# Stores issued from the ScalarE queue instead of the SyncE queue, in a recurrence with a highway layer behind it

## The chip, the cores and the metric

The kernel runs on one core of one Trainium2 chip. The metric is the device time of one launch in microseconds (us); less is better. A core has TensorE (PE in the profile), VectorE (DVE), ScalarE (ACT), GpSimd (POOL) and SyncE (SP), each with its own instruction stream that runs in order, and 16 DMA engines that move data between HBM and on-chip memory. A DMA is started by an instruction on some engine's stream; here that is SP or ACT.

## The reference

Two layers over 25344 tokens (4 sequences of 6336) of 256 channels, float32 in and out:

```python
sig = 1.0 / (1.0 + np.exp(-f_logit))
f = lower_bound + (1.0 - lower_bound) * sig
i = 1.0 - f
for t in range(S):                      # per sequence, per channel
    h = f[:, t] * h + i[:, t] * x[:, t]
    y[:, t] = h
# second layer, on y as (25344, 256)
H = np.maximum(y @ w_h, 0.0)
T = 1.0 / (1.0 + np.exp(-(y @ w_t + b_t)))
out = T * H + (1.0 - T) * y
```

Both inputs, `x` and `f_logit`, are read once and the output is written once: 26 MB each.

## The kernel before

The tokens are cut into 21 units, numbered 0 to 20, of 2 to 16 blocks of 128 tokens; a unit of 16 blocks has two halves of 8 (sub-tiles). Each block group goes through one chain:

- `l` and `x` load the logits and the inputs (1 MB for 8 blocks), into 5 buffers each (slots 0 to 4).
- `u` (ACT) is the sigmoid of the negated logits; `b`/`B` (POOL, in two cases DVE) multiplies it by `x`. A slot of `l` is free when its `u` is done, a slot of `x` when its product is done.
- `i` and `p` (PE) transpose both; `f` (ACT, in some cases DVE) makes the gate; `s` (DVE) is the scan over time.
- `z` and `g` (PE) are the two matrix products, `t` (ACT) the second sigmoid, `d` (DVE) and `e`/`E` (POOL or DVE) the gating.
- `o` (PE) puts the result for 4 blocks in PSUM, `c` (ACT, in three cases DVE) copies it to one of 4 buffers `o`, and `w` stores that buffer: 512 KB, in three cases 256 KB.

A token such as `w7.0.1` is the store of unit 7, chunk 0, half 1; `l11.1` is the load of the logits of unit 11, sub-tile 1; `:3` behind a token names its slot or bank. The whole order of the work is one string of tokens written by hand, and every engine runs its own tokens in that order. So the place of a `w` token sets where the store stands in the stream of the engine that issues it. `do_w` (L408) issues stores and `load` (L250) issues loads; both go to SP before the change, 51 stores and 58 loads on one queue.

The program gives every DMA one of eight completion counters, shown as DMAHW0 to DMAHW7, in turn over the DMAs of all queues. A DMA that takes a counter first waits until the DMA that had it before, eight DMAs earlier, has landed. We call the counters lanes.

Of the kernel before, what the change touches and what calls it, by code (L numbers as in the profile page):

```python
# [55 lines left out]
b4.0.0:1 o1.0.0:1 p3.0.0:5 k*4:6 s3.1:0 l6.0:1 c0.0.0:0 x6.0:1 i4.0.1:4 f4.1:0 b4.0.1 k*4:0 k*4:0 s3.0:1 i4.0.0:0
l7.1:2 g3.0.1:67 d2.0.1 e2.0.1 c1.0.0v:1 w1.0.0 d3.0.1:3 u5.0:1 i5.0.1:2 p4.0.0:1 B5.0:2 i5.0.0:3 z3.0.0:45 f4.0:3
f5.1:2 f5.0:1 g3.0.0:67 z3.0.1:23 t3.0.0:0 w0.0.0 x7.1:2 s4.0:2 p4.0.1:0 p5.0.0:1 o2.0.0:45 u6.0:2 d3.0.0 e3.0.0
l7.0:3 t3.0.1 x7.0:3 c2.0.0:2 i6.0.1:6 f6.1:3 s4.1:3 g4.0.1:23 p5.0.1:0 u7.1:3 e3.0.1v d4.0.1:0 o3.0.1:45 c3.0.1:3
z4.0.1:67 t4.0.1:1 o3.0.0:23 z4.0.0:45 s5.0:4 i6.0.0:1 b6.0.1:0 c3.0.0:1 t4.0.0 g4.0.0:67 s5.1:5 g5.0.1:23 d4.0.0  # L60
b6.0.0 p6.0.0:0 z5.0.1:67 l8.0:4 f6.0:0 u7.0:0 t5.0.1:2 w3.0.1 l8.1:0 b7.1.1:1 x8.1:4 d5.0.1:1 z5.0.0:45 s6.0:0 t5.0.0
i7.0.1:23 i7.1.1 f7.1:1 b7.1.0 e4.0.1 e4.0.0v p6.0.1:1 s6.1:1 w2.0.0 g5.0.0:67 x8.0:0 o4.0.0:45 c4.0.0:0 g6.0.1:23
u8.0:1 l9.1:1 o4.0.1:45 p7.1.1:01 d5.0.0 b7.0.0:2 d6.0.1:2 c4.0.1:3 b7.0.1 p7.0.1 l9.0:2 e5.0.0v i7.0.0:67 e5.0.1
w3.0.0 u8.1:2 i7.1.0 s7.1:2 f7.0:2 p7.0.0:45 p7.1.0 z6.0.0:23 x9.0:1 z6.0.1:67 t6.0.0:0 t6.0.1 i8.0.1:01 s7.0:3 i8.1.1
# [5 lines left out]
E7.1 d8.0.0:2 w6.0.0 w6.0.1 x10.0:4 s9.1:0 b10.1.1:2 o7.0.1:45 u10.0:1 b10.1.0 o7.0.0:67 c7.0.1:1 c7.0.0:2 i10.0.0  # L70
p9.1.0:45 p9.0.0 s9.0:1 z8.0.1:67 l11.1:0 o7.1.1:23 f10.0:0 l11.0:2 t8.0.1:0 c7.1.1:3 z8.1.1:01 b10.0.1:0 x11.1:0
w7.0.0 t8.1.1:1 i10.0.1:67 i10.1.1 o7.1.0:23 g8.0.1:01 w7.0.1 c7.1.0v:0 z8.1.0:45 d8.0.1 f10.1:3 x11.0:1 t8.1.0
b10.0.0 g9.1.1:23 z9.1.1:67 g9.0.0:45 w7.1.1 u11.1:3 d9.1.1:3 t9.1.1:2 z8.0.0:23 t8.0.0 u11.0:0 E8.1v d9.0.0:0
g9.0.1:01 d9.0.1 w7.1.0 p10.1.0:67 z9.0.0:45 p10.0.0 l12.0:1 e8.0.1 z9.0.1:23 e8.0.0v t9.0.0:1 t9.0.1 o8.1.1:01
c8.1.1:2 i11.0.1:45 i11.1.1 p10.1.1:23 p10.0.1 f11.1:2 o8.0.0:01 c8.0.0:1 s10.0:2 o8.0.1:67 b11.1.0:1 i11.0.0:45
b11.1.1 l12.1:3 i11.1.0 b11.0.0:2 c8.0.1:3 x12.1:2 b11.0.1 f11.0:1 s10.1:3 o8.1.0:01 u12.0:2 c8.1.0:0 e9.1.1 g9.1.0:67
d9.1.0 g10.1.1:23 d10.1.1:2 g10.0.0:45 d10.0.0:1 w8.1.1 e9.0.1 g10.1.0:67 d10.1.0 g10.0.1:23 u12.1:1 d10.0.1
z10.0.0:01 e9.0.0 t10.0.0:0 e10.0.0v p11.0.0:45 z10.0.1:67 t10.0.1 p11.1.0 o9.0.1:23 c9.0.1:2 z10.1.0:01 t10.1.0:1
x12.0:3 l20.0:4 b12.1.0:0 z10.1.1:67 t10.1.1 e10.0.1 w8.0.1 l13.0:0 w8.1.0 w8.0.0 i12.1.1:23 i12.0.1 f12.1:0 w9.0.1
l13.1:2 s11.0:4 p11.1.1:01 p11.0.1 e10.1.0v x13.0:4 e10.1.1 s11.1:5 o9.0.0:67 c9.0.0:3 w9.0.0 z9.1.0:45 o10.0.1:23  # L80
i12.0.0:67 t9.1.0 c10.0.1:0 i12.1.0 w10.0.1 b12.0.1:1 o10.0.0:45 b12.0.0 b12.1.1 f12.0:3 o10.1.0:23 c10.1.0:1
c10.0.0:2 g11.1.1:01 d11.1.1:0 g11.0.1:67 d11.0.1:1 e9.1.0 g11.0.0:23 d11.0.0 x13.1:0 w10.0.0 u13.0:3 b13.0.0:2
u13.1:0 b13.0.1 g11.1.0:01 o10.1.1:45 d11.1.0 p12.0.0:67 c10.1.1:3 p12.1.0 s12.0:2 z11.0.0:23 z11.1.1:01 o9.1.1:45
t11.1.1:0 t11.0.0:1 e11.0.0 p12.0.1:01 u20.0:2 p12.1.1 i13.0.0:23 i13.1.0 c9.1.1:0 l14.0:1 x14.0:1 f13.0:1 o9.1.0:67
l15.0:3 s12.1:3 w10.1.1 w9.1.1 b13.1.1:1 z11.1.0:45 i13.1.1:23 w10.1.0 t11.1.0 c9.1.0:2 l16.0:0 e11.1.1v i13.0.1
f13.1:2 w9.1.0 e11.1.0v z11.0.1:45 t11.0.1 b13.1.0 g12.1.0:67 d12.1.0:2 g12.0.0:01 u14.0:1 d12.0.0:3 e11.0.1
g12.1.1:23 z12.1.0:67 x15.0:3 p13.0.0:45 p13.1.0 t12.1.0:2 d12.1.1 z12.0.0:01 t12.0.0:0 z12.1.1:23 t12.1.1 b14.0.0:0
e12.1.1 o11.1.1:67 c11.1.1:3 x16.0:2 s13.0:0 e12.1.0 w11.1.1 o11.0.1:01 c11.0.1:0 p13.0.1:23 p13.1.1 i14.0.1:6 f14.1:3
w11.0.1 e12.0.0 o11.1.0:45 c11.1.0:1 s13.1:1 w11.1.0 z12.0.1:01 t12.0.1 o11.0.0:67 c11.0.0:2 g12.0.1:45 d12.0.1
o12.1.0:01 w11.0.0 i14.0.0:6 f14.0v:0 b14.0.1 u15.0:3 z13.0.1:23 t13.0.1:1 g13.1.1:45 u16.0:0 g13.0.1:67 b15.0.1:2  # L90
d13.1.1:0 z13.1.0:23 t13.1.0:2 o12.1.1:45 c12.1.1:3 x17.0:4 c12.1.0:0 d13.0.1:1 g13.1.0:67 l17.0:2 e12.0.1v o12.0.0:23
c12.0.0:1 e13.0.1v b15.0.0 p14.0.1:4 i16.0.1:5 b16.0.0:1 f16.1:1 p14.0.0:0 d13.1.0 e13.1.0 i15.0.1:1 f15.1:2 s14.1:4
l18.0:4 o12.0.1:67 c12.0.1:2 z13.1.1:23 s14.0:5 w12.0.1 t13.1.1 w12.1.0 w12.1.1 g13.0.0:45 i16.0.0:1 f16.0:3 e13.1.1
d13.0.0 z13.0.0:67 w12.0.0 p15.0.1:0 s15.1:2 z14.0.0:23 t13.0.0 i15.0.0:1 t14.0.0:0 g14.0.0:67 g14.0.1:45 d14.0.0:2
e13.0.0 d14.0.1 z14.0.1:23 p15.0.0:0 f15.0:0 b16.0.1 s15.0:3 u17.0:1 t14.0.1 i20.0.1:1 f20.1:2 o13.1.1:67 x18.0:0
E14.0v o13.0.0:45 c13.1.1:2 c13.0.0:0 o13.0.1:23 x19.0:1 g15.0.1:01 c13.0.1:3 u18.0:3 d15.0.1:3 B17.0:0 p16.0.1:6
g15.0.0:45 o13.1.0:23 d15.0.0 c13.1.0:1 i17.0.1:0 s16.1:0 w13.0.1 f17.1:0 p16.0.0:1 z15.0.1:45 z15.0.0:23 w13.0.0
t15.0.1:2 b18.0.1:2 t15.0.0 p17.0.1:0 o14.0.0:67 c14.0.0:3 s16.0:1 o14.0.1:45 c14.0.1:0 w13.1.1 i18.0.0:2 i17.0.0:1
f17.0:1 f18.0:3 l19.0:1 x20.0:3 g16.0.0:67 z16.0.0:45 t16.0.0:1 s17.1:4 u19.0:0 d16.0.0:1 g16.0.1:01 d16.0.1 p17.0.0:3
z16.0.1:67 E15.0 o15.0.0:45 o15.0.1:12 s17.0:5 w14.0.0 i20.0.0:0 f20.0v:0 w13.1.0 t16.0.1 c15.0.0:2 b18.0.0 p18.0.0:6  # L100
i18.0.1:7 c15.0.1:3 b20.0.0:1 f18.1:1 g17.0.0:45 z17.0.1:23 s18.0:2 z17.0.0:01 t17.0.1:0 d17.0.0:0 i19.0.0:6 p18.0.1:7
s18.1:3 t17.0.0 f19.0:3 E16.0 B19.0:0 g17.0.1:23 o16.0.0:45 c16.0.0:1 e17.0.0 w14.0.1 o16.0.1:01 c16.0.1:0 d17.0.1
g18.0.0:67 z18.0.0:45 t18.0.0:2 d18.0.0:2 p19.0.0:0 s19.0:0 w15.0.1 w15.0.0 i19.0.1:1 g18.0.1:23 f19.1:1 z18.0.1:67
p19.0.1:0 t18.0.1 w16.0.1 w16.0.0 p20.0.0:1 e17.0.1 d18.0.1 o17.0.0:45 o17.0.1:23 s19.1:1 g19.0.1:0 c17.0.0:3 w17.0.0
e18.0.0 e18.0.1v p20.0.1:4 c17.0.1:2 w17.0.1 d19.0.1:3 z19.0.1:5 o18.0.1:67 z19.0.0:0 s20.0:4 s20.1:5 t19.0.1:1
c18.0.1:0 t19.0.0 g19.0.0:1 w18.0.1 o18.0.0:23 c18.0.0:1 e19.0.1 d19.0.0 g20.0.1:4 z20.0.0:0 z20.0.1:1 t20.0.1:0
e19.0.0v t20.0.0 o19.0.0:67 w18.0.0 c19.0.0:3 g20.0.0:2 w19.0.0 d20.0.1:1 d20.0.0 e20.0.1 e20.0.0v o20.0.0:0 c20.0.0:2
w20.0.0
"""

    pool = ctx.enter_context(tc.tile_pool(name="sb", bufs=1))
# [296 lines left out]
    def do_w(eng, slot, n, q, r):  # L408
        j0, j1 = blocks(n, q, r)
        o = st[n]["o", q, r].rearrange("p (j d) -> p j d", d=D)  # L410
        pin(nc.sync.dma_start(rows(out, units[n][0], j0, j1), o[:, :j1 - j0]))
# [40 lines left out]
```

## Time and profile before

| | |
|---|---|
| time, median of 3 runs | 208.13 us (208.1 to 209.46) |
| the profiled execution | 208.83 us |
| its span, first to last instruction | 207.1 us |
| busy: PE, DVE, ACT, POOL | 194.7, 192.8, 190.9, 171.9 us |
| moved by DMA | 78.67 MB, mean 380 GB/s |
| granted TensorE clock | 1.0 throughout |

All times in the views below are us from the span's start, if no other unit is given. A row of the timeline gives start, length, engine, line, operation and the tiles that it writes and reads; "SPq" and "ACTq" are the instruction streams (sequencers) of those engines, whose waits and DMA issues are not counted as busy time. "x2" means two like instructions that follow each other, merged into one row with their joint length.

### The profile page before, as it was taken

What the parts mean: (1) busy time and instruction counts of PE and PEld (TensorE: products, weight loads), DVE (VectorE), ACT (ScalarE), POOL (GpSimd) and SP (SyncE); (2) the same over time, 40 slices, a digit from 0 to 9 for tenths busy, and PEclk for the clock granted to TensorE, in tenths of its full rate; (3) what the DMA queues carried; (4) which work ended last, traced back from release to release, by engine and by line L of the source; (5) the groups of instructions that cost most, each with busy time, mean ns of one, the idle gap of its engine ahead of it and who ended that gap; (6) DMA issues with size and microseconds to landing.
All of it is one profiled execution on the core that took longest, in us unless ns stands there. A gap on an engine that the chain in (4) does not pass through costs nothing.

```text
span 207.1 us, 4606 instructions
## 1 busy us (share of the span) xinstructions
PE 194.7 (94%) x1850; PEld 135.0 (65%) x1850; DVE 192.8 (93%) x141; ACT 190.9 (92%) x173; POOL 171.9 (83%) x90
## 2 busy tenths in 40 slices
...
GB/s 178 365 425 416 418 423 418 418 419 412 425 418 420 420 419 421 424 417 419 427 415 418 423 414 429 418 417 427 412 424 390 403 325 352 364 141 161 206 304 253
DMA packets 15980, 78.67 MB, mean 380 GB/s; under 512 B 1748, under 2 KB 2264, under 8 KB 10072
## 3 DMA queue, kind: packets, MB, share of 16 engines
q1 hardware_dynamic: 15952, 78.39, 93.5%
...
q14 instruction: 6, 0.05, 0.1%
...
## 4 chain that ended last, share of the span: by engine, by line
PE 48%; DVE 17%; ACT 16%; DMA 11%; issue 4%; POOL 2%; SPq 1%; DVEq 0%; ACTq 0%
PE psum L333 13%; PE psum L145 11%; DMA l<-in_f_logit_dram 11%; DVE y L320 10%; PE psum L393 6%; DVE d L363 6%; PE psum L394 6%; ACT f L301 6%; PE psum L286 6%; PE psum L311 5%; ACT u L262 4%; ACT t L356 3%; ACT o L405 2%; POOL bv L277 2%; DVE f L299 1%
## 5 line engine op out<-in xcount | busy, mean ns | idle before, releaser
L277 POOL TENSOR_TENSOR bv<-u,x 128x1024 bf16<-128x1024 f16 (+2 forms) x44 | 99.8, 2293 | 18.3 <-ACT f L301 7.4
L320 DVE TENSOR_TENSOR_SCAN y<-f,y,psum 128x1024 bf16<-128x1024 f16 (+6 forms) x40 | 103.7, 2614 | 1.0 <-ACT f L301 0.6
L377 POOL TENSOR_TENSOR d<-d,t 128x1024 bf16<-128x1024 bf16 (+3 forms) x35 | 71.7, 2063 | 11.4 <-ACT t L356 6.1
L333 PE MATMUL psum<-y,w_sb 128*128 128x512 bf16 (+1 forms) x224 | 77.4, 367 | 3.0 <-ACT f L301 1.9
L145 PE MATMUL psum<-y,w_sb 128*128 128x512 bf16 x184 | 69.7, 379 | 0.7 <-DVE y L320 0.7
L363 DVE SCALAR_TENSOR_TENSOR d<-y,ncc,psum 128x1024 bf16<-128x1024 bf16 (+2 forms) x56 | 62.6, 1147 | 3.4 <-PE psum L145 1.5
L356 ACT ACTIVATE t<-psum,bt 128x1024 bf16<-128x1024 f32 (+2 forms) x56 | 56.3, 1038 | 2.6 <-PE psum L145 1.7
L262 ACT ACTIVATE u<-l 128x2048 f16<-128x2048 f32 (+2 forms) x28 | 48.6, 1747 | 5.4 <-DMA l<-in_f_logit_dram 5.4
L301 ACT ACTIVATE f<-psum,ncc 128x1024 f16<-128x1024 f16 (+3 forms) x38 | 50.9, 1365 | 1.6 <-PE psum L286 1.6
L405 ACT COPY o<-psum 128x1024 f32<-128x1024 f32 (+1 forms) x49 | 48.5, 1031 | 2.2 <-PE psum L394 1.0
L393 PE MATMUL psum<-diag,y 128*128 128x128 f16 x396 | 48.8, 219 | 0.6 <-ACT f L301 0.4
L394 PE MATMUL psum<-ident_b,d 128*128 128x128 bf16 x396 | 48.6, 219 | 0.8 <-DVE d L377 0.8
L394 PEld LDWEIGHTS <-d 128*128 128x128 bf16 x396 | 44.0, 113 | 4.8 <-DVE d L377 1.2
L393 PEld LDWEIGHTS <-y 128*128 128x128 bf16 x396 | 44.2, 113 | 2.5
L333 PEld LDWEIGHTS <-w_sb 128*128 128x128 f16 x224 | 21.6, 98 | 18.1 <-issue 1.0
L145 PEld LDWEIGHTS <-w_sb 128*128 128x128 f16 x184 | 17.9, 97 | 21.3 <-issue 6.0
L311 PE MATMUL psum<-ident_f,bv 128*128 128x128 f32 x198 | 29.3, 276 | 1.3 <-POOL bv L277 0.8
L286 PE MATMUL psum<-ident_h,u 128*128 128x128 f16 x396 | 28.6, 219 | 1.2 <-ACT u L262 0.8
L286 PEld LDWEIGHTS <-u 128*128 128x128 f16 x396 | 25.0, 98 | 6.9 <-ACT u L262 2.1
L311 PEld LDWEIGHTS psum<-ident_f,bv 128*128 128x128 f32 x198 | 22.4, 141 | 7.1 <-POOL bv L277 2.1
L377 DVE TENSOR_TENSOR d<-d,t 128x1024 bf16<-128x1024 bf16 (+3 forms) x15 | 10.6, 718 | 0.2
L145 PE MATMUL psum<-zeros 128*128 128x512 bf16 x39 | 10.6, 399 | 0.0
...
## 6 DMA issues: line engine op xcount, KB each, us to landing
out_dram<-o SPq DMA_DIRECT2D x48, 512.0 KB, 7.9
l<-in_f_logit_dram SPq DMA_DIRECT2D x23, 1024.0 KB, 14.6
x<-in_x_dram SPq DMA_DIRECT2D x23, 1024.0 KB, 14.4
l<-in_f_logit_dram SPq DMA_DIRECT2D x2, 512.0 KB, 5.9
x<-in_x_dram SPq DMA_DIRECT2D x2, 512.0 KB, 7.4
...
```

The lines of the kernel that those rows point to most:

```text
L145: return pe.add_instruction(mybir.InstMatmult(name=nc.get_next_instruction_name(), start_tensor_calc=start, stop_tensor_calc=stop, tile_si ...
L277: shared(pin(e.tensor_mul(st[n]["bv", s][:, a:c].rearrange("p k d j -> p k j d"), st[n]["u", s][:, 2 * a:2 * c].rearrange("p (k j) d -> p ...
L286: pin(nc.tensor.transpose(uT[:, j * P:(j + 1) * P], st[n]["u", s][:, j, h * P:(h + 1) * P], ident_h))
L301: pin(nc.scalar.activation(to, of, AF.Identity, scale=ncc[:, h:h + 1], bias=1.0))
L311: pin(nc.tensor.transpose(words[:, k:k + g * (P - 1) + 1:g], pair, ident_f))
L320: pin(nc.vector.tensor_tensor_scan(y[:, c:e], st[n]["f", h][:, c:e], data, 0.0 if fresh else carry[h], op0=ALU.mult, op1=ALU.add))
L333: pin(nc.tensor.matmul(p.part(a, e), w, data, start=ki == 0, stop=ki == NH - 1))
L356: pin(nc.scalar.activation(half(n, q, "t", m), z, AF.Sigmoid, bias=bt[:, m:m + 1]))
L363: pin(nc.vector.scalar_tensor_tensor(half(n, q, "d", m), y, ncc[:, m:m + 1], g, op0=ALU.mult, op1=ALU.max))
L377: shared(pin(e.tensor_mul(d, d, t)), not eng)
L393: pin(nc.tensor.matmul(o, st[n]["y", h][:, whole], diag[:, h], start=True, stop=False))
L394: pin(nc.tensor.matmul(o, half(n, q, "d", h)[:, cols], ident_b, start=False, stop=True))
```

## The change

The last 13 stores stay on SP, where by that time no load is left behind them. The 38 stores ahead of them get an `a` at the end of their token, which sends them to ACT's queue, and a new place in the string: behind the token that follows their copy on ACT. The order of all other tokens is as before.

```diff
     def do_w(eng, slot, n, q, r):
         j0, j1 = blocks(n, q, r)
         o = st[n]["o", q, r].rearrange("p (j d) -> p j d", d=D)
-        pin(nc.sync.dma_start(rows(out, units[n][0], j0, j1), o[:, :j1 - j0]))
+        queue = nc.scalar if eng else nc.sync
+        pin(queue.dma_start(rows(out, units[n][0], j0, j1), o[:, :j1 - j0]))
...
-        name = token.rstrip("v")
+        name = token.rstrip("av")
...
-            here["do_" + name[0]](token.endswith("v"), slot, *[int(c) for c in name[1:].split(".")])
+            here["do_" + name[0]](token[-1] in "av", slot, *[int(c) for c in name[1:].split(".")])
```

Two lines of the string of tokens before, and what stands in their place now:

```diff
-i8.0.0:23 w4.0.0 g6.0.0:67 x9.1:2 d6.0.0 f8.1:0 i8.1.0 f8.0:3 o5.0.0:01 c5.0.0:2 g7.0.0:45 d7.0.0:3 u9.0:0 g7.1.1:23
-d7.1.1:0 B8.1:0 p8.1.1:67 u9.1:3 g7.0.1:01 d7.0.1 o5.0.1:45 c5.0.1:1 B8.0:2 p8.0.1 s8.1:4 z7.0.1:23 t7.0.1:1 z7.1.1:01
...
+t6.0.1 i8.0.1:01 s7.0:3 i8.1.1 i8.0.0:23 g6.0.0:67 x9.1:2 d6.0.0 f8.1:0 i8.1.0 f8.0:3 o5.0.0:01 c5.0.0:2 g7.0.0:45
+d7.0.0:3 u9.0:0 w5.0.0a g7.1.1:23 d7.1.1:0 B8.1:0 p8.1.1:67 u9.1:3 g7.0.1:01 d7.0.1 o5.0.1:45 c5.0.1:1 B8.0:2 p8.0.1
+s8.1:4 z7.0.1:23 t7.0.1:1 w5.0.1a z7.1.1:01 z7.0.0:45 t7.1.1:2 t7.0.0 p8.1.0:23 p8.0.0 E6.0 o6.0.1:01 c6.0.1:0
```

The first place is where units 7 to 12 meet, from about 73 to 92 us of the profiled execution. SP before the change: the loads l11.1, l11.0 and x11.1, the stores w7.0.0 and w7.0.1, the load x11.0, the stores w7.1.1 and w7.1.0, the loads l12.0 and l12.1.

```order
L250 DMA l<-in_f_logit_dram 128x2048 [waits DMAHW5_49]
L250 DMA l<-in_f_logit_dram 128x2048 [waits DMAHW6_49]
L250 DMA x<-in_x_dram 128x2048 [waits DMAHW7_49,Pool_49]
L411 DMA out_dram<-o 128x1024 [waits DMAHW0_49,Activation_49]
L411 DMA out_dram<-o 128x1024 [waits DMAHW1_49]
L250 DMA x<-in_x_dram 128x2048 [waits DMAHW2_49,Pool_49]
L411 DMA out_dram<-o 128x1024 [waits DMAHW3_49,Activation_49]
L411 DMA out_dram<-o 128x1024 [waits DMAHW4_49,DVE_49]
L250 DMA l<-in_f_logit_dram 128x2048 [waits DMAHW5_49]
L250 DMA l<-in_f_logit_dram 128x2048 [waits DMAHW6_49]
```

Each load behind a store stands here behind that store's wait for its copy (Activation or DVE). SP after the change, same place: l11.1, l11.0, x11.1, x11.0, l12.0, l12.1, x12.1, x12.0, l20.0.

```order
L250 DMA l<-in_f_logit_dram 128x2048 [waits DMAHW3_49,Activation_49]
L250 DMA l<-in_f_logit_dram 128x2048 [waits DMAHW4_49,Activation_49]
L250 DMA x<-in_x_dram 128x2048 [waits DMAHW6_49,Pool_49]
L250 DMA x<-in_x_dram 128x2048 [waits DMAHW2_49,DMAHW0_49,Pool_49]
L250 DMA l<-in_f_logit_dram 128x2048 [waits DMAHW7_49,DMAHW1_49,Activation_49]
L250 DMA l<-in_f_logit_dram 128x2048 [waits DMAHW5_49,DMAHW2_49,Activation_49]
L250 DMA x<-in_x_dram 128x2048 [waits DMAHW4_49,Pool_49]
L250 DMA x<-in_x_dram 128x2048 [waits DMAHW6_49,Pool_49]
L250 DMA l<-in_f_logit_dram 128x512 [waits DMAHW7_49,Activation_49]
```

The stores are gone from SP, and the loads now wait for their own slot (Activation: the `u`; Pool: the product) and lane; the lane that a load takes is the last DMAHW of its row, so l11.1 has lane 3, x11.0 lane 0 and l12.0 lane 1. ACT after the change, same place: the copies c7.0.1 and c7.0.0, then the stores w7.0.1, w7.0.0, w7.1.1 and w7.1.0 with the work between them.

```order
L405 COPY o<-psum 128x1024 [waits DMAHW2_49,PE_49]
L405 COPY o<-psum 128x1024 [waits DVE_49,PE_49]
L412 DMA out_dram<-o 128x1024 [waits DMAHW3_49,Activation_49]
L301 ACTIVATE f<-psum,ncc 128x2048 [waits PE_49]
L412 DMA out_dram<-o 128x1024 [waits DMAHW5_49,Activation_49]
L356 ACTIVATE t<-psum,bt 128x1024 [waits PE_49,Pool_49]
L405 COPY o<-psum 128x1024 [waits DMAHW7_49,DVE_49,PE_49]
L356 ACTIVATE t<-psum,bt 128x1024 [waits PE_49,Pool_49]
L412 DMA out_dram<-o 128x1024 [waits DMAHW0_49,Activation_49]
L301 ACTIVATE f<-psum,ncc 128x2048 [waits PE_49]
L356 ACTIVATE t<-psum,bt 128x1024 [waits DVE_49,PE_49]
L412 DMA out_dram<-o 128x1024 [waits DMAHW1_49,DVE_49]
```

Before, ACT had no store between these operations; now w7.0.1 takes lane 3 behind l11.1, w7.1.1 lane 0 behind x11.0, w7.1.0 lane 1 behind l12.0, and each waits on ACT until that load has landed. w7.0.0, on lane 5, follows the store w6.0.1.

The second place is from about 143 to 150 us of the profiled execution. ACT after the change: the copies c11.1.1 and c11.0.1 with the store w11.1.1 behind them, an `f`, the store w11.0.1, the copy c11.1.0, a `t`, the store w11.1.0, the copy c11.0.0, a `u`, the store w11.0.0.

```order
L405 COPY o<-psum 128x1024 [waits DMAHW4_49,PE_49]
L405 COPY o<-psum 128x1024 [waits DMAHW7_49,PE_49]
L412 DMA out_dram<-o 128x1024 [waits Activation_49]
L301 ACTIVATE f<-psum,ncc 128x1024 [waits PE_49]
L412 DMA out_dram<-o 128x1024 [waits DMAHW6_49,Activation_49]
L405 COPY o<-psum 128x1024 [waits DMAHW0_49,DVE_49,PE_49]
L356 ACTIVATE t<-psum,bt 128x1024 [waits PE_49]
L412 DMA out_dram<-o 128x1024 [waits DMAHW0_49,Activation_49]
L405 COPY o<-psum 128x1024 [waits DMAHW2_49,PE_49]
L262 ACTIVATE u<-l 128x2048 [waits Pool_49]
L412 DMA out_dram<-o 128x1024 [waits DMAHW1_49,Activation_49]
```

These four stores stood on SP before; now each stands between two operations of ACT, w11.0.1 on lane 6, w11.1.0 on lane 0, w11.0.0 on lane 1. SP after the change, same place: the loads x16.0, x17.0, l17.0, l18.0 and x18.0.

```order
L250 DMA x<-in_x_dram 128x2048 [waits DMAHW5_49,Pool_49]
L250 DMA x<-in_x_dram 128x2048 [waits DMAHW6_49,Pool_49]
L250 DMA l<-in_f_logit_dram 128x2048 [waits DMAHW0_49,Activation_49]
L250 DMA l<-in_f_logit_dram 128x2048 [waits DMAHW7_49,DMAHW1_49,Activation_49]
L250 DMA x<-in_x_dram 128x2048 [waits DMAHW3_49,Pool_49]
```

Before, SP had the four stores ahead of x17.0, l17.0 and l18.0; now nothing of theirs stands there, and these three loads hold lanes 6, 0 and 1, for which the stores on ACT wait.

More of the change, by code (lines that the diff above doesn't have):

```diff
@@ L55 @@
 g2.0.0:1 d2.0.0:2 z2.0.0:0 t2.0.0:2 g2.0.1:3 k*1:2 o0.0.0:2 p3.0.1:0 l5.0:0 u4.0:0 z2.0.1:4 t2.0.1 e2.0.0 x5.0:0
[L56 to L64, printed above, removed]
@@ L65 @@
-i8.0.0:23 w4.0.0 g6.0.0:67 x9.1:2 d6.0.0 f8.1:0 i8.1.0 f8.0:3 o5.0.0:01 c5.0.0:2 g7.0.0:45 d7.0.0:3 u9.0:0 g7.1.1:23
-d7.1.1:0 B8.1:0 p8.1.1:67 u9.1:3 g7.0.1:01 d7.0.1 o5.0.1:45 c5.0.1:1 B8.0:2 p8.0.1 s8.1:4 z7.0.1:23 t7.0.1:1 z7.1.1:01
-w4.0.1 z7.0.0:45 t7.1.1:2 t7.0.0 p8.1.0:23 p8.0.0 E6.0 o6.0.1:01 c6.0.1:0 o6.0.0:67 c6.0.0:3 b9.0.0:1 z7.1.0:45
-i9.0.0:01 b9.0.1 i9.1.0 b9.1.0:0 g7.1.0:67 t7.1.0 b9.1.1 l10.1:3 s8.0:5 l10.0:4 f9.0:1 i9.1.1:45 e7.0.1 u10.1:2 w5.0.1
-d7.1.0 e7.0.0 g8.1.1:23 d8.1.1:1 x10.1:3 g8.1.0:01 d8.1.0 i9.0.1 f9.1:2 w5.0.0 g8.0.0:67 p9.1.1:23 p9.0.1 i10.1.0:01
@@ L70 @@
[L70 to L108, printed above, removed]
+b4.0.0:1 o1.0.0:1 p3.0.0:5 k*4:6 s3.1:0 l6.0:1 c0.0.0:0 x6.0:1 i4.0.1:4 f4.1:0 w0.0.0a b4.0.1 k*4:0 k*4:0 s3.0:1
+i4.0.0:0 l7.1:2 g3.0.1:67 d2.0.1 e2.0.1 c1.0.0v:1 d3.0.1:3 u5.0:1 i5.0.1:2 p4.0.0:1 B5.0:2 i5.0.0:3 z3.0.0:45 f4.0:3
@@ new lines @@
+w1.0.0a f5.1:2 f5.0:1 g3.0.0:67 z3.0.1:23 t3.0.0:0 x7.1:2 s4.0:2 p4.0.1:0 p5.0.0:1 o2.0.0:45 u6.0:2 d3.0.0 e3.0.0
+l7.0:3 t3.0.1 x7.0:3 c2.0.0:2 i6.0.1:6 f6.1:3 w2.0.0a s4.1:3 g4.0.1:23 p5.0.1:0 u7.1:3 e3.0.1v d4.0.1:0 o3.0.1:45
+c3.0.1:3 z4.0.1:67 t4.0.1:1 w3.0.1a o3.0.0:23 z4.0.0:45 s5.0:4 i6.0.0:1 b6.0.1:0 c3.0.0:1 t4.0.0 w3.0.0a g4.0.0:67
+s5.1:5 g5.0.1:23 d4.0.0 b6.0.0 p6.0.0:0 z5.0.1:67 l8.0:4 f6.0:0 u7.0:0 t5.0.1:2 l8.1:0 b7.1.1:1 x8.1:4 d5.0.1:1
+z5.0.0:45 s6.0:0 t5.0.0 i7.0.1:23 i7.1.1 f7.1:1 b7.1.0 e4.0.1 e4.0.0v p6.0.1:1 s6.1:1 g5.0.0:67 x8.0:0 o4.0.0:45
@@ new lines @@
+c4.0.0:0 g6.0.1:23 u8.0:1 w4.0.0a l9.1:1 o4.0.1:45 p7.1.1:01 d5.0.0 b7.0.0:2 d6.0.1:2 c4.0.1:3 b7.0.1 p7.0.1 l9.0:2
+e5.0.0v i7.0.0:67 e5.0.1 u8.1:2 w4.0.1a i7.1.0 s7.1:2 f7.0:2 p7.0.0:45 p7.1.0 z6.0.0:23 x9.0:1 z6.0.1:67 t6.0.0:0
+t6.0.1 i8.0.1:01 s7.0:3 i8.1.1 i8.0.0:23 g6.0.0:67 x9.1:2 d6.0.0 f8.1:0 i8.1.0 f8.0:3 o5.0.0:01 c5.0.0:2 g7.0.0:45
+d7.0.0:3 u9.0:0 w5.0.0a g7.1.1:23 d7.1.1:0 B8.1:0 p8.1.1:67 u9.1:3 g7.0.1:01 d7.0.1 o5.0.1:45 c5.0.1:1 B8.0:2 p8.0.1
+s8.1:4 z7.0.1:23 t7.0.1:1 w5.0.1a z7.1.1:01 z7.0.0:45 t7.1.1:2 t7.0.0 p8.1.0:23 p8.0.0 E6.0 o6.0.1:01 c6.0.1:0
@@ new lines @@
+o6.0.0:67 c6.0.0:3 w6.0.1a b9.0.0:1 z7.1.0:45 i9.0.0:01 b9.0.1 i9.1.0 b9.1.0:0 g7.1.0:67 t7.1.0 w6.0.0a b9.1.1 l10.1:3
+s8.0:5 l10.0:4 f9.0:1 i9.1.1:45 e7.0.1 u10.1:2 d7.1.0 e7.0.0 g8.1.1:23 d8.1.1:1 x10.1:3 g8.1.0:01 d8.1.0 i9.0.1 f9.1:2
+g8.0.0:67 p9.1.1:23 p9.0.1 i10.1.0:01 E7.1 d8.0.0:2 x10.0:4 s9.1:0 b10.1.1:2 o7.0.1:45 u10.0:1 b10.1.0 o7.0.0:67
+c7.0.1:1 c7.0.0:2 w7.0.1a i10.0.0 p9.1.0:45 p9.0.0 s9.0:1 z8.0.1:67 l11.1:0 o7.1.1:23 f10.0:0 w7.0.0a l11.0:2 t8.0.1:0
+c7.1.1:3 z8.1.1:01 b10.0.1:0 x11.1:0 t8.1.1:1 w7.1.1a i10.0.1:67 i10.1.1 o7.1.0:23 g8.0.1:01 c7.1.0v:0 z8.1.0:45
@@ new lines @@
+d8.0.1 f10.1:3 x11.0:1 t8.1.0 w7.1.0a b10.0.0 g9.1.1:23 z9.1.1:67 g9.0.0:45 u11.1:3 d9.1.1:3 t9.1.1:2 z8.0.0:23 t8.0.0
+u11.0:0 E8.1v d9.0.0:0 g9.0.1:01 d9.0.1 p10.1.0:67 z9.0.0:45 p10.0.0 l12.0:1 e8.0.1 z9.0.1:23 e8.0.0v t9.0.0:1 t9.0.1
+o8.1.1:01 c8.1.1:2 i11.0.1:45 i11.1.1 p10.1.1:23 p10.0.1 f11.1:2 w8.1.1a o8.0.0:01 c8.0.0:1 s10.0:2 o8.0.1:67
+b11.1.0:1 i11.0.0:45 b11.1.1 l12.1:3 i11.1.0 b11.0.0:2 c8.0.1:3 w8.0.0a x12.1:2 b11.0.1 f11.0:1 w8.0.1a s10.1:3
+o8.1.0:01 u12.0:2 c8.1.0:0 e9.1.1 g9.1.0:67 d9.1.0 g10.1.1:23 d10.1.1:2 g10.0.0:45 d10.0.0:1 e9.0.1 g10.1.0:67 d10.1.0
@@ new lines @@
+g10.0.1:23 u12.1:1 w8.1.0a d10.0.1 z10.0.0:01 e9.0.0 t10.0.0:0 e10.0.0v p11.0.0:45 z10.0.1:67 t10.0.1 p11.1.0
+o9.0.1:23 c9.0.1:2 z10.1.0:01 t10.1.0:1 w9.0.1a x12.0:3 l20.0:4 b12.1.0:0 z10.1.1:67 t10.1.1 e10.0.1 l13.0:0
+i12.1.1:23 i12.0.1 f12.1:0 l13.1:2 s11.0:4 p11.1.1:01 p11.0.1 e10.1.0v x13.0:4 e10.1.1 s11.1:5 o9.0.0:67 c9.0.0:3
+z9.1.0:45 o10.0.1:23 i12.0.0:67 t9.1.0 w9.0.0a c10.0.1:0 i12.1.0 b12.0.1:1 o10.0.0:45 b12.0.0 b12.1.1 f12.0:3 w10.0.1a
+o10.1.0:23 c10.1.0:1 c10.0.0:2 w10.1.0a g11.1.1:01 d11.1.1:0 g11.0.1:67 d11.0.1:1 e9.1.0 g11.0.0:23 d11.0.0 x13.1:0
```

26 lines of the change are left out of this document (added).

## The prediction

> **What bounds the kernel now.** I read the page first: the busy shares, the slices, the DMA rows.
>
> ```profile
> PE 194.7 (94%) x1850; PEld 135.0 (65%) x1850; DVE 192.8 (93%) x141; ACT 190.9 (92%) x173; POOL 171.9 (83%) x90
> q1 hardware_dynamic: 15952, 78.39, 93.5%
> l<-in_f_logit_dram SPq DMA_DIRECT2D x23, 1024.0 KB, 14.6
> out_dram<-o SPq DMA_DIRECT2D x48, 512.0 KB, 7.9
> ```
>
> Four resources lie between 92 and 94% of the span, and a load lands 14.6 us after its issue, so several are always queued. The table by stages says where each is full.
>
> ```profile
> core 0: us, PE busy (x) PEld busy (x) DVE busy (x) ACT busy (x) POOL busy (x), PEclk, DMA share, GB/s
> 26.00:90.00 64.00, 59.01 (x568) 41.10 (x567) 62.85 (x36) 63.59 (x51) 61.22 (x26) 1.00 1.02 420
> 90.00:150.00 60.00, 58.65 (x581) 41.84 (x579) 58.83 (x35) 59.30 (x49) 55.10 (x27) 1.00 1.02 420
> 150.00:181.00 31.00, 30.85 (x308) 22.07 (x307) 30.68 (x21) 30.98 (x32) 26.53 (x12) 1.00 0.97 376
> 181.00:207.10 26.10, 21.60 (x236) 15.97 (x234) 20.18 (x20) 19.90 (x24) 17.04 (x9) 1.00 0.54 214
> ```
>
> From 26 to 150 us the DMA engines are full (share 1.02, 420 GB/s: 2.50 us for a 1 MB load, 1.25 us for a 512 KB store), and ACT is busy 63.59 of 64, 59.30 of 60 and, to 181 us, 30.98 of 31 us. Whatever is added to ACT in those stages, or makes it wait, moves everything behind it. The waits of ACT from 26 us on, and those of SP:
>
> ```profile
> ACT t L356 <- PE psum L145: 1.7, 4, 0.8
> ACT o L405 <- PE psum L394: 1.0, 3, 0.6
> ACT u L262 <- DMA l<-in_f_logit_dram: 0.8, 1, 0.8
> SPq L411 <- ACT o L405: 95.0, 30, 8.5
> ```
>
> ACT waits for a load once, 0.8 us. SP waits 95 us at stores for their copies: it does nothing else, and the full DMA engines show that this costs nothing as long as loads are queued.
>
> **The change part by part.** *Removed from SP:* 38 of 51 issues and most of those 95 us. Since the DMA engines were full through 150 us, freeing SP gives them nothing there: 0 us.
>
> *Added to ACT, the issues.* The length of one, and what ACT's stream does meanwhile:
>
> ```profile
> L411 SPq DMA_DIRECT2D out_dram<-o x51: 332/344/1867, 26.4 to 204.1; - x51
> 1.31 1.28 ACT L154 ACT_TABLE_LOAD   x1 [1.31 <-PEq L436]
> 1.38 0.24 ACTq L168 DMA_DIRECT2D prm<-in_moe_b_t_dram  x1
> L405 ACTq EVENT_SEMAPHORE  x51: 17/38/3192, 37.3 to 201.7; - x51
> ```
>
> An issue takes 0.34 us on SP. On ACT, L168 was issued at 1.38 us inside the table load of 1.31 to 2.59, so an issue can run under an operation already handed to the engine. Each store has such cover, the operation behind its copy, of at least 1.0 us. Bounds: 0 (all covered) to 38 x 0.34 = 12.9 us (none covered). I take 0, since L168 is the one row of the thing itself. If the cover is gone (the issue starts after it ends), the price is 0.34 us each.
>
> *Added to ACT, the lanes.* ACT's stream is in order: the last row shows it held up to 3.2 us at a wait ahead of a copy. While a store waits there for its lane, nothing behind it is handed over, and ACT idles once the cover ends; PE waits behind it for `f`, `t` and free banks, DVE for PE, POOL for `t`. On SP this wait was free. So I ask, for each store whose lane was held by a load, when that load lands and when ACT would have gone on. Three loads and ACT's rows of that place:
>
> ```profile
> L250 SPq DMA_DIRECT2D l<-in_f_logit_dram x1: 328/328/328, 56.6 to 56.6; - x1
> DMA to landing us min/median/max: 16.1/16.1/16.1
> L250 SPq DMA_DIRECT2D l<-in_f_logit_dram x1: 480/480/480, 73.2 to 73.2; - x1
> DMA to landing us min/median/max: 14.3/14.3/14.3
> L250 SPq DMA_DIRECT2D x<-in_x_dram x1: 382/382/382, 83.0 to 83.0; - x1
> DMA to landing us min/median/max: 14.4/14.4/14.4
> 71.74 1.12 ACT L356 ACTIVATE t<-psum,bt 128x1024 bf16<-128x1024 f32 x1
> 81.98 1.98 ACT L301 ACTIVATE f<-psum,ncc 128x2048 f16<-128x2048 f16 x1
> 86.74 2.01 ACT L301 ACTIVATE f<-psum,ncc 128x2048 f16<-128x2048 f16 x1
> 89.87 1.90 ACT L262 ACTIVATE u<-l 128x2048 f16<-128x2048 f32 x1
> ```
>
> The loads are l10.1 (lands at 72.7), l11.1 (87.5) and x11.0 (97.4). With full DMA engines a load can't land earlier than the bytes ahead of it allow, and these are the same after the change: the same loads stand ahead of x11.0, and 13 stores before (those that SP issued up to 83 us, w7.0.0 and w7.0.1 the last) as now (all up to w7.0.0). So:
>
> - w6.0.1 (lane 5, behind l10.1): two more stores, w5.0.0 and w5.0.1, are now ahead of l10.1: 72.7 + 2.5 = 75.2. With 0.34 for the issue, the `t` at 71.74 begins at 75.5: ACT is 3.8 us late.
> - w7.0.1 (lane 3, behind l11.1; 11 stores ahead, before and now): 87.5 + 0.34, where the `f` began at 81.98: 5.9 us late in all.
> - w7.1.1 (lane 0, behind x11.0): 97.4 + 0.34, where the `f` began at 86.74: 11.0 us late in all. It includes the two above and any early loss: whatever came first, ACT can't be earlier here.
> - w7.1.0 (lane 1, behind l12.0, next on SP): 97.4 + 2.5, or 3.75 with w7.1.1 between, + 0.34 against 89.87: 10.4 to 11.6, so at most another 0.6; I take 0.3.
>
> From there ACT runs 11 us behind the DMA engines, and the loads are ahead. Does the lateness grow? The rows near the end:
>
> ```profile
> L250 SPq DMA_DIRECT2D l<-in_f_logit_dram x1: 718/718/718, 149.1 to 149.1; - x1
> DMA to landing us min/median/max: 12.5/12.5/12.5
> 147.19 1.02 ACT L405 COPY o<-psum 128x1024 f32<-128x1024 f32 x1
> 143.40 5.17 SPq L411 DMA_DIRECT2D out_dram<-o  x4
> ```
>
> The load is l17.0 (161.6), on whose lane w11.1.0 waits; ACT went on at 147.19. By that landing the lateness would be 161.6 + 0.34 - 147.2 = 14.7 us. But four stores were ahead of it on SP, and ACT, 11 us late, has issued at most one of them by then: 3 or 4 x 1.25 us less, 9.7 to 11.0. I take no growth, and 14.7 as the bound.
>
> *Given back.* After 181 us ACT idles 26.1 - 19.9 = 6.2 us, waiting for PE and for the end. A late ACT can use little of it, as PE and DVE are late with it. Bounds: 0 to the 3.5 us of the three waits above; I take 1.0.
>
> **Sum**, on the profiled execution's 208.83 us (span 207.1, and 1.7 around it): + 11.0 + 0.3 + 0 (issues) - 1.0 = 219.1. The execution was 0.7 us above the median of 208.13, so 218.4; I say **219 us**. Low end: stores that share the DMA engines poorly let x11.0 pass two of them (8.5 late) and 3.5 given back, so 208.1 + 5 = 213. High end: 14.7 late, or issues uncovered, 227 below.
>
> The Trainium skill, page "DMA: Bandwidth & Descriptors", section "Queues, rings and completion order", states that each DMA engine takes turns between the rings of the queues that have work. No run here shows two busy rings yet; by it a store passes queued loads, as I assume for w5.0.0 and w5.0.1.
>
> **Rivals.**
>
> *No change.* The bytes and the DMA engines are the same, and ACT always reaches the lanes late enough. For it: full DMA engines from 26 to 150 us. Against: the 86.74 and 97.4 above, 10.7 us apart; a landing would have to come that much earlier. Time: 208. The same page, section "Issuing engines are not separate DMA queues", says that issuing from several engines saves only the sequencer's issue time; by that rule the time stays. The rule has nothing on a wait that moves to a busy engine.
>
> *Faster.* SP no longer holds loads behind copies. Where DMA isn't full, 150 to 181 us, the lost rate is worth 31 x (420 - 376)/420 = 3.2 us, and the last loads land that much sooner: 205. Against: ACT is busy 30.98 of those 31 us and waits 0.8 us for loads in all, so little can come of it.
>
> *Slower still: no cover.* If ACT issues only when its pipeline is empty, or the queue is slow to take the DMA (the longest issue on SP took 1.87 us), each store costs 0.34 us. Up to w7.1.1 that vanishes in the wait for x11.0, which sets the time there; the 24 stores behind it add 24 x 0.34 = 8.2: 227. L168 speaks against it.
>
> **How the numbers follow.** Lanes as worked out: 0.66. No cover: 0.17. No change: 0.12. Faster: 0.05. The range of 212 to 228 takes in the first two with their bounds and leaves out 0.17. The measurement tells about 1% from no change: faster 0.05, same 0.12, slower 0.66 + 0.17 = 0.83.
>
> **What the profile after would show.** ACT's longest waits stand at the `f` behind w7.1.1, released by DMA x, with ACT some 11 us behind at the `u` of 89.87 (near 101); the copies near 147 are no further behind; ACT's busy time stays at 191 us with 11 us more idle; stores land sooner than 7.9 us; SP's 95 us are mostly gone. ACT with many gaps of 0.3 us, one behind each cover, would show the no-cover case. ACT reaching 89.87 on time would prove the forecast wrong.

## The result, and the profile after

The changed kernel takes 219.78 us (median of 4 runs, 219.05 to 220.71), the kernel before, on the same chip, 208.12 us (207.9 to 209.46): a ratio of 1.055, 95% interval 1.049 to 1.061. The profiled execution took 219.81 us, with a span of 218.0 us against 207.1. First the page of the changed kernel: busy times, the two DMA queues (SP's is q1, ACT's q10) and the DMA issues with their median time to landing.

```profile
PE 197.3 (90%) x1850; PEld 136.8 (63%) x1850; DVE 193.4 (89%) x141; ACT 191.6 (88%) x173; POOL 172.1 (79%) x90
q1 hardware_dynamic: 10480, 58.99, 66.5%
q10 hardware_dynamic: 5480, 19.40, 22.0%
l<-in_f_logit_dram SPq DMA_DIRECT2D x23, 1024.0 KB, 16.6
out_dram<-o ACTq DMA_DIRECT2D x36, 512.0 KB, 8.5
```

ACT's work is the same (191.6 us), so the 10.9 us of span are waits. The stages (busy time of PE, PEld, DVE, ACT and POOL in each, then clock, DMA share and rate):

```profile
26.00:90.00 64.00, 55.35 (x521) 39.38 (x520) 59.42 (x34) 58.89 (x46) 59.65 (x25) 0.97 1.02 422
90.00:150.00 60.00, 54.45 (x502) 36.84 (x501) 52.46 (x32) 54.22 (x44) 46.32 (x23) 0.97 1.01 413
150.00:181.00 31.00, 30.92 (x326) 22.72 (x325) 30.72 (x21) 30.94 (x31) 26.73 (x14) 1.00 0.78 313
```

The waits of ACT and of SP over the whole execution (total, times, longest), with ACT's waits for loads from 26 us on in the last row:

```profile
ACT u L262 <- DMA l<-in_f_logit_dram: 7.0, 7, 2.6
ACT f L301 <- DMA x<-in_x_dram: 4.4, 1, 4.4
SPq L250 <- DMA l<-in_f_logit_dram: 47.5, 11, 9.1
SPq L250 <- DMA x<-in_x_dram: 36.1, 12, 4.6
SPq L412 <- ACT o L405: 34.9, 8, 15.0
ACT u L262 <- DMA l<-in_f_logit_dram: 3.1, 4, 1.6
```

ACT, busy 63.59 of 64 us before, is now busy 58.89; from 90 to 150 us it was 59.30 and is 54.22. From 150 to 181 us it is full again: the loss lies ahead of that. From 26 us on ACT waits 3.1 us for loads, 0.8 before (the rest of the 7.0 us lies ahead of that, while the first loads come in), and once 4.4 us at an `f`. This largest piece in ACT's own timeline, some rows of it, where the prediction put it:

```profile
87.28 0.34 ACTq L412 DMA_DIRECT2D out_dram<-o  x1
87.67 1.97 ACT L301 ACTIVATE f<-psum,ncc 128x2048 f16<-128x2048 f16 x1 [1.19 <-PE psum L145]
91.43 1.14 ACT L356 ACTIVATE t<-psum,bt 128x1024 bf16<-128x1024 f32 x1
96.60 0.34 ACTq L412 DMA_DIRECT2D out_dram<-o  x1
96.99 1.97 ACT L301 ACTIVATE f<-psum,ncc 128x2048 f16<-128x2048 f16 x1 [4.43 <-DMA x<-in_x_dram]
99.64 0.34 ACTq L412 DMA_DIRECT2D out_dram<-o  x1
100.03 1.91 ACT L262 ACTIVATE u<-l 128x2048 f16<-128x2048 f32 x1
```

The store in the fourth row is w7.1.1. Between 92.57, when the `t` ends, and 96.99 ACT has nothing to do; its next operation, the `f` that began at 86.74 before, stands behind that store, and the store waits for an x load, x11.0. An `f` needs no x: the releaser shown is the lane's. The `u` of 89.87 begins at 100.03. Operation by operation, ACT is 10.2 us late there, 11.05 us at 129.1 and 10.9 us at its end.

### The profile page after: what moved, and what is told of

Its sections match the earlier page's. It is cut to its first block, busy times and chain, and to the rows that moved or that the text cites. A ratio compares the mean times of both kernels' runs of the same rounds, so it can differ in the third digit from the quotient of the medians.

```text
span 218.0 us, 4608 instructions
## 1 busy us (share of the span) xinstructions
PE 197.3 (90%) x1850; PEld 136.8 (63%) x1850; DVE 193.4 (89%) x141; ACT 191.6 (88%) x173; POOL 172.1 (79%) x90
## 4 chain that ended last, share of the span: by engine, by line
DMA 47%; PE 32%; DVE 9%; ACT 6%; issue 3%; POOL 2%; SPq 1%; ACTq 0%; DVEq 0%; POOLq 0%
DMA x<-in_x_dram 39%; PE psum L333 10%; PE psum L145 8%; DVE y L320 6%; DMA out_dram<-o 5%; PE psum L393 4%; PE psum L394 4%; PE psum L311 3%; DMA l<-in_f_logit_dram 3%; PE psum L286 2%; ACT o L405 2%; ACT f L301 2%; DVE d L363 2%; POOL bv L277 2%; ACT u L262 1%
## 5 line engine op out<-in xcount | busy, mean ns | idle before, releaser
L301 ACT ACTIVATE f<-psum,ncc 128x1024 f16<-128x1024 f16 (+3 forms) x38 | 50.6, 1355 | 8.9 <-DMA x<-in_x_dram 4.4
L393 PE MATMUL psum<-diag,y 128*128 128x128 f16 x396 | 49.7, 221 | 1.0 <-ACT o L405 0.5
L394 PE MATMUL psum<-ident_b,d 128*128 128x128 bf16 x396 | 49.6, 221 | 0.8 <-DVE d L377 0.8
L394 PEld LDWEIGHTS <-d 128*128 128x128 bf16 x396 | 44.5, 114 | 4.9 <-issue 1.4
L311 PE MATMUL psum<-ident_f,bv 128*128 128x128 f32 x198 | 29.9, 280 | 1.0 <-POOL bv L277 0.6
L311 PEld LDWEIGHTS psum<-ident_f,bv 128*128 128x128 f32 x198 | 23.1, 144 | 6.3 <-POOL bv L277 1.5
## 6 DMA issues: line engine op xcount, KB each, us to landing
l<-in_f_logit_dram SPq DMA_DIRECT2D x23, 1024.0 KB, 16.6
```

Source lines behind the costliest of these rows:

```text
L301: pin(nc.scalar.activation(to, of, AF.Identity, scale=ncc[:, h:h + 1], bias=1.0))
L311: pin(nc.tensor.transpose(words[:, k:k + g * (P - 1) + 1:g], pair, ident_f))
L393: pin(nc.tensor.matmul(o, st[n]["y", h][:, whole], diag[:, h], start=True, stop=False))
L394: pin(nc.tensor.matmul(o, half(n, q, "d", h)[:, cols], ident_b, start=False, stop=True))
```

## Experiments

The theories: (1) lane waits on ACT; (2) the issues on ACT; (3) stores on a second queue pass loads, and the loads come late; (4) the new place of the stores in the string; and, formed after the first four runs, (5) output buffers.

**place_only and queue_only: half of the change each.**

```diff
-        queue = nc.scalar if eng else nc.sync
+        queue = nc.sync
```

That is place_only: the new string, all stores on SP. In queue_only the string is that of before, with an `a` at the same 38 stores.

> All 38 stores at the new places in the string, but all issued by SP. Theory 1 (ACT stands in its own stream at a store until the load that holds the store's lane has landed): SP waits there instead, which costs ACT nothing; 208 to 211 us, ACT's waits at L301 released by a DMA gone. Theory 2 (the issues cost ACT 0.34 us each): no issue on ACT, 208 us. Theory 3 (a second queue lets stores pass queued loads, so that loads land late): one queue again, 208 us. Theory 4 (not the queue but the new place of the stores in the string costs the time): 219 us as in the changed kernel.

> The string of the kernel before, place for place; only the queue of the same 38 stores is ACT. Theory 1: the lanes are dealt another way, w7.0.1 stands behind x11.0 at the same f (86.74 us of the kernel before), which lands near 96 to 97, so 9.5 to 11 us late there, and later lanes behind l17.0 or l18.0 can make it up to 14 us; 218 to 222 us. Theories 2 and 3: the same 38 issues and the same second queue, 219 us. Theory 4 (the place): 208 us.

Measured: place_only 225.92 us (ratio 1.084, 1.079 to 1.089), queue_only 232.88 us (1.115, 1.110 to 1.121). Neither half alone is harmless, and each is worse than both together; no theory had that. Waits of ACT and SP in place_only, then of ACT in queue_only:

```profile
ACT u L262 <- DMA l<-in_f_logit_dram: 11.5, 10, 3.9
ACT o L405 <- DMA out_dram<-o: 7.4, 3, 3.7
SPq L412 <- ACT o L405: 151.5, 39, 11.2
```

```profile
ACT o L405 <- DMA out_dram<-o: 12.9, 6, 4.0
ACT u L262 <- DVE o L403: 2.6, 1, 2.6
```

The new place puts a store right behind its copy. On SP it holds the loads behind it until the copy is done (151.5 us of such waits, 95.0 before), so loads come late to `u` (7.6 of the 11.5 us fall after 26 us). The old place is late in the string: on SP that lets loads go first, on ACT it leaves a finished buffer waiting behind other operations, and copies wait 12.9 us for buffers (the first time 2.35 us at the copy of 50.6 us of the kernel before, ahead of any lane wait that theory 1 had named). The second row is a store that waits in ACT's stream for its copy on DVE, and the `u` behind it with it. Where a store stands right behind its own copy on ACT, nothing covers its issue, and ACT idles, here 0.47 us:

```profile
133.40 0.34 ACTq L412 DMA_DIRECT2D out_dram<-o  x1
133.84 1.11 ACT L356 ACTIVATE t<-psum,bt 128x1024 bf16<-128x1024 f32 x1 [0.47 <-ACT o L405]
```

So queue and place belong together, and these two runs can't tell how the changed kernel itself loses its time.

**w67_on_sp and safe: lanes freed in part and in full.** The first puts the six stores w6.0.1 to w7.1.0 back on SP, at which ACT had come to be 10 us late; the second puts back eight others, so that no store on ACT finds its lane held. Two of the six, by way of example (`a` taken off, old place):

```diff
-g8.0.0:67 p9.1.1:23 p9.0.1 i10.1.0:01 E7.1 d8.0.0:2 x10.0:4 ...
+g8.0.0:67 p9.1.1:23 p9.0.1 i10.1.0:01 E7.1 d8.0.0:2 w6.0.0 w6.0.1 x10.0:4 ...
```

> The changed kernel with the six stores of units 6 and 7 back on SP at their old places; 32 stores stay on ACT. These six are the ones at which the changed kernel loses its first 10 us. Theory 1 with the rule that every lane counts: ACT is at most 3 us late at the u of 89.87 us, but the next stores whose lanes are held by loads (w9.1.0 behind l16.0, w11.1.0 behind l17.0, w12.0.0 behind x19.0, landing 9 to 17 us after ACT would go on by the landings of before, and 5 to 10 us by those of the changed kernel) hold it from 130 us on: 214 to 220 us in all. Theory 1 with only these places: 208 to 211 us. Theories 2 and 3: 32/38 of 11.7, 218 us, the loss spread evenly over the span instead of arising after 130 us.

> 30 of the 38 stores on ACT at their new places, 8 (w6.0.0, w7.0.0, w7.1.0, w9.0.1, w9.1.1, w9.1.0, w11.0.0, w13.0.1) on SP at their old ones. The 8 are chosen so that every store on ACT takes a lane whose last DMA, by the landings of the kernel before, has landed at least 1.1 us before ACT gets there. Theory 1: no store holds ACT, 208 to 210.5 us. Theory 2 (issues): 30 of 38 issues, 208.1 + 11.7 x 30/38 = 217 us. Theory 3 (stores passing loads): about 30/38 of the loss too, 217 us. Theory 4 (place): 217 us.

Measured: w67_on_sp 219.01 us (1.050, 1.046 to 1.054), safe 219.30 us (1.052, 1.048 to 1.057). In w67_on_sp the `u` of 89.87 begins at 91.72, 1.85 us late instead of 10.2: the six stores did make the loss there. It comes back between 130 and 160 us, as theory 1 said when every lane counts, at a copy whose buffer isn't free and then behind stores on ACT whose lanes loads hold, here w9.1.0 (third row) behind l16.0:

```profile
91.72 1.90 ACT L262 ACTIVATE u<-l 128x2048 f16<-128x2048 f32 x1
139.05 1.01 ACT L405 COPY o<-psum 128x1024 f32<-128x1024 f32 x1 [3.08 <-DMA out_dram<-o]
143.29 0.34 ACTq L412 DMA_DIRECT2D out_dram<-o  x1
143.68 1.11 ACT L356 ACTIVATE t<-psum,bt 128x1024 bf16<-128x1024 f32 x1 [1.74 <-DMA l<-in_f_logit_dram]
```

Safe contradicts theory 1 as I had it: no lane holds ACT, it is 2.2 us late up to 131 us, and still it ends 10.3 us late. What it waits for most, beside loads:

```profile
ACT o L405 <- DMA out_dram<-o: 5.6, 2, 3.7
```

One of the two, in the timeline:

```profile
139.67 1.01 ACT L405 COPY o<-psum 128x1024 f32<-128x1024 f32 x1 [3.70 <-DMA out_dram<-o]
```

The store it waited for, w10.0.0 (its issue, and who waited for its landing):

```profile
L412 ACTq DMA_DIRECT2D out_dram<-o x1: 339/339/339, 125.0 to 125.0; - x1
  ACT o L405: 3.7, 1
```

Issued at 125.0 us, it gave its buffer back only near 139.7, 14.7 us later, where the same store took 7.5 us before. Two loads, l14.0 and x14.0, were issued at 118.8 and 119.8, ahead of it; before, l14.0 was issued at 123.2, behind it. SP, with fewer stores to wait at, runs ahead with loads, this store queues behind more bytes, and four output buffers are too few. That is theory 5; in the changed kernel it would stand behind the lane waits.

The two waits for buffers are 5.6 of the 8.0 us that ACT loses in safe after 131 us. The other 2.4 us follow at two `t`, which wait for PE:

```profile
147.01 1.11 ACT L356 ACTIVATE t<-psum,bt 128x1024 bf16<-128x1024 f32 x1 [1.66 <-PE psum L145]
148.75 1.11 ACT L356 ACTIVATE t<-psum,bt 128x1024 bf16<-128x1024 f32 x1 [0.62 <-PE psum L145]
```

PE had been at half its clock from 139 to 146 us, behind the first wait for a buffer; the last section has the rows.

**after_o5 and safe_o5: a fifth output buffer under both.** Only slot numbers of copies change, as here:

```diff
-c4.0.0:0 g6.0.1:23 u8.0:1 w4.0.0a l9.1:1 o4.0.1:45 p7.1.1:01 d5.0.0 b7.0.0:2 d6.0.1:2 c4.0.1:3 ...
+c4.0.0:0 g6.0.1:23 u8.0:1 w4.0.0a l9.1:1 o4.0.1:45 p7.1.1:01 d5.0.0 b7.0.0:2 d6.0.1:2 c4.0.1:1 ...
```

> The changed kernel with five output buffers instead of four (one more 4 KB per partition, copies take them in turn); stores, places and lanes as in the changed kernel. Theory 1 (lanes): the stores wait for their lanes as before, ACT is still 10 us late at the u of 89.87 us; 218.5 to 220 us. Theory 5 (SP, freed, lets loads run ahead, stores land later, and the copies wait for one of four output buffers; the lane waits only stand in front of that): 211 to 213 us.

> The kernel with 30 stores on ACT whose lanes are free (run safe), with five output buffers instead of four. Theory 1 with theory 5 as a second limit behind it: neither lanes nor buffers hold ACT; what is left is the 2.2 us that loads came late up to 75 us; 210 to 212.5 us. Theory 2 (issues, 30 x 0.34 us) or theory 4 (the place): 217 to 219 us, as with four.

Measured: after_o5 219.43 us (1.053, 1.049 to 1.057), safe_o5 211.07 us (1.013, 1.009 to 1.017). The two by two:

| | 4 buffers | 5 buffers |
|---|---|---|
| lanes held (the change) | 219.78 | 219.43 |
| lanes free | 219.30 | 211.07 |

Lifting either limit alone gains 0.5 or 0.35 us, less than the spread of the changed kernel's runs (219.05 to 220.71); lifting both gains 8.7, and with five buffers, freeing the lanes alone is worth 8.4. (The lower row also has eight stores back on SP.) So the lane waits set the time of the changed kernel, as predicted, but an equal loss stood behind them. In safe_o5 ACT has no wait on a DMA but these, 2.8 us of them from 26 us on:

```profile
ACT u L262 <- DMA l<-in_f_logit_dram: 7.2, 8, 2.1
```

**pad1: a lane moved by one.** A load of 64 bytes, which nothing reads, ahead of x12.0:

```diff
-... t10.1.0:1 w9.0.1a x12.0:3 l20.0:4 ...
+... t10.1.0:1 w9.0.1a n x12.0:3 l20.0:4 ...
+    def do_n(slot):
+        pads.append(sb([1, 16], FP32, f"pad{len(pads)}x"))
+        pin(nc.sync.dma_start(pads[-1], lower_bound[:16].rearrange("(a b) -> a b", a=1)))
```

> The changed kernel with one more DMA, a load of 64 bytes that nothing reads, on SP ahead of x12.0. It shifts the lanes by one from there on: w7.1.0 now takes the lane of l12.1 (landed at 102.85 us in the changed kernel) instead of that of l12.0 (99.56). Theory 1: ACT goes on 3.3 us later at the u of 89.87 us, 13.3 us late; 221.5 to 223 us, or less by what the later lanes then give back. All other theories: 64 bytes change nothing, 219.8 us.

Measured: 222.87 us (1.069, 1.064 to 1.075).

```profile
102.35 0.34 ACTq L412 DMA_DIRECT2D out_dram<-o  x1
102.73 1.91 ACT L262 ACTIVATE u<-l 128x2048 f16<-128x2048 f32 x1 [3.34 <-DVE d L363]
```

The `u` of 89.87 begins at 102.73, 12.9 us late, 2.7 later than in the changed kernel; 64 bytes cost 3.1 us. DVE, named as releaser, is not it: the store ahead, w7.1.0, was issued at 102.35 and ended the wait. This is the most direct proof of theory 1: same stores, same places, same bytes but 64, another lane for this store (and for the DMAs behind the pad).

**early: stores that find their lanes free, and the loads beside them.** The nine stores to w5.0.1 on ACT, the rest as before:

> Only the nine stores up to w5.0.1 on ACT, at their new places; all later ones on SP at their old places. None of the nine finds its lane held late. Theory 3 as a small part (stores on a second queue pass queued loads, so that the loads up to 75 us land 2 us later): ACT 2 to 2.5 us late from the u of 62 us on and no more after it, 210 to 211 us. If passing costs nothing: 208 us. Theory 2 (9 issues): 208.1 + 9 x 0.34 = 211 us, spread evenly from 23 to 67 us instead of arising at the u.

Measured: 211.15 us (1.014, 1.009 to 1.019). ACT is 2.4 us late at the `u` that began at 62.06, 1.8 of it new there, and 2.1 at its end:

```profile
64.49 1.92 ACT L262 ACTIVATE u<-l 128x2048 f16<-128x2048 f32 x1 [1.74 <-DMA l<-in_f_logit_dram]
```

The load that this `u` reads, l9.0, and behind it a store on the other queue, w4.0.1:

```profile
L250 SPq DMA_DIRECT2D l<-in_f_logit_dram x1: 328/328/328, 49.4 to 49.4; - x1
DMA to landing us min/median/max: 15.0/15.0/15.0
L412 ACTq DMA_DIRECT2D out_dram<-o x1: 339/339/339, 52.3 to 52.3; - x1
DMA to landing us min/median/max: 9.2/9.2/9.2
```

The load is issued at 49.4 and lands at 64.4; the store, issued 2.9 us after it, lands at 61.5, ahead of it. In the kernel before, l9.0 landed at 61.5, 2.9 us sooner. Passing need not be the whole of this: l9.0 itself was issued 5.7 us later than before (at 43.7), when l8.0, which had its lane, had landed (49.3), and w3.0.0 was issued at 40.7 instead of 46.2, so that it now stood ahead of l9.0. How the 2.9 us divide, this run doesn't show.

**late24_o5, before_o5, place_only_o5: does it add up?** The first has 24 stores on ACT, none early, none with a held lane or buffer; the others add the fifth buffer to the kernel before and to place_only.

> 24 stores on ACT at their new places, none of them before w6.0.1; the nine early ones and w6.0.0, w9.0.1, w9.1.1, w11.0.0 and w12.0.1 on SP at their old places; five output buffers. The 24 are chosen so that no store finds its lane held and no copy its buffer. Theories 1, 3 and 5 together: none of the three losses is left, 207.5 to 209.5 us. Theory 2 (24 issues x 0.34 us): 216 us. If stores on a second queue cost something of themselves beside these three: 211 us and more.

> The kernel before with five output buffers instead of four. Its copies never waited for a buffer, so nothing changes: 208 us, within 0.5%. If the fifth buffer were worth time of itself (as it would have to be, if it and not the lifted waits explained the 8 us between the runs safe and safe_o5): 200 to 206 us.

> The run place_only (all stores on SP at the new places, 225.9 us) with five output buffers. Its ACT waited 11.5 us for loads, which SP held behind stores that waited for their copies, and 7.4 us for output buffers. If these are two losses that add: 217 to 220 us, late by 6 us from the u of 74.6 us on. If the late loads make the late buffers: 224 to 226 us.

Measured: late24_o5 209.02 us (1.0045, 1.0023 to 1.0067), before_o5 208.62 us (1.0018, 0.9996 to 1.0039), place_only_o5 219.42 us (1.053, 1.051 to 1.055). The fifth buffer is worth nothing by itself. With the three losses avoided, 24 issues on ACT cost about 0.9 us in all, 1.4 by the end of the interval, where 0.34 us each would be 8.2; its issues and its only waits for a DMA, all of them ahead of 26 us:

```profile
L412 ACTq DMA_DIRECT2D out_dram<-o x24: 338/339/384, 69.8 to 170.0; - x24
ACT u L262 <- DMA l<-in_f_logit_dram: 3.9, 5, 1.2
```

place_only loses 6.5 of its 17.7 us with the fifth buffer, so late loads and late buffers were two losses there. No version is faster than the kernel before.

## Why the prediction was right, point by point

- **The cause.** Lane waits on ACT, 219 against a measured 219.78. Shown by pad1 (lanes moved by one, +3.1 us), w67_on_sp (six stores taken off ACT, 8.3 us less delay at the `u` of 89.87) and after_o5 against safe_o5 (lanes freed where buffers are no limit, 8.4 us).
- **The chain of delays.** Predicted 3.8 us at the `t` of 71.74, 5.9 at the `f` of 81.98, 11.0 at the `f` of 86.74, 0.3 more behind l12.0. ACT was 4.5, 5.7, 10.25 and, at the `u` of 89.87 behind l12.0, 10.15 us late. The first step was right in its number by luck: w6.0.1 found its lane free, for l10.1 had landed at 73.9 and the store was issued at 75.4, once its copy was done. Of the 4.5 us, 3.0 arose by the `u` of 62.06, where loads came late (see early), and 1.5 at the copies of 69.91 and 70.83, the first of which waited 1.5 us for PE, then at half its clock (last section); the prediction had neither. Both are gone in the total because, as the prediction said of x11.0, whatever came first, ACT can't be earlier there. The next two steps are lane waits as predicted, of 1.2 and 4.4 us.
- **No growth after that.** Right as to the lanes. But ACT, 10.15 us late at the `u` of 89.87, was 11.05 late at 129.1 for reasons that the prediction didn't have: 0.3 us at the `t` of 92.67, and 0.5 at a copy, 0.35 of it a wait for its output buffer. It was 11.3 us late at most and 10.9 at the end. So the 11.3 of the sum was met, but 10.2 of it by the lanes.
- **Issues at nothing.** Right where the cover is there: late24_o5 puts 24 of them at about 0.9 us in all, 1.4 at most by its interval. Without cover one cost 0.47 us of idle time in queue_only, somewhat more than the 0.34 us that the rival "no cover" put on it.
- **Given back, 1.0 us.** Mis-sized: after 181 us of the kernel before nothing came back, ACT was 10.95 us late there and 10.9 at the end. So 219.1 stood against the 219.81 us of the profiled execution. That 219 then met the median of 219.78 so closely is partly luck: the lanes came out 1.1 us below the sum's 11.3, and 0.8 us of growth and the 1.0 that didn't come back made up for it.
- **Removed from SP, 0 us.** Wrong in its reason, though it cost the sum nothing. Full DMA engines meant no gain, but SP's waits had a use: they kept loads behind stores. Without them the same 38 stores landed sooner after their issue, 8.3 us in the median instead of 9.4, as the prediction expected (its 7.9 is the median of all stores of 512 KB, the last 12 among them). The loads landed later, `l` 16.6 us after its issue instead of 14.6, and from 26 us on ACT's `u` waited 3.1 us for them instead of 0.8. SP's 95 us at copies shrank to 34.9, and its loads now wait 83.6 us for older loads to land (47.5 + 36.1). The landings of the 38 stores, before and after (least, median, most):

```profile
DMA to landing us min/median/max: 4.7/9.4/16.6
DMA to landing us min/median/max: 2.8/8.3/12.3
```

- **The rival "no change", 208 us.** Its price was wrong. It said that with the lanes free the time would stay. Safe has the lanes free and takes 219.30: the waits for buffers, and the slower PE behind them, cost nearly the same. The forecast would have come out right even if its mechanism hadn't been there.
- **The rule on issuing engines.** Moving nine issues to ACT, and with them their places, made early 1.4% slower, with none of them held by a lane. The Trainium skill, "DMA: Bandwidth & Descriptors", section "Issuing engines are not separate DMA queues", has several issuing engines save sequencer time and nothing else; early differs from it.
